# Local attention's weighted sums of V: from VectorE products and halvings to TensorE matmuls with softmax weights laid out as bands

## The chip, the cores and the metric

The kernel runs on one core of a Trainium2 chip. The metric is the device time of one execution in microseconds. Times of profiled executions come with a trace, from which the profile is made; TensorE's granted clock is 1.000 in the profile of the kernel before.

## The reference, cut to what matters

The output is a gated mix of two branches that read the same input `x` of 2048 tokens by 1024 features, in bf16.

```python
g = _sigmoid((x * gate_w).sum(-1, keepdims=True))
a = _A_ref(x, A_wqkv, A_wo)        # local dilated attention
b = _B_ref(x, B_w_gate, B_w_up, B_w_down)   # gelu(x w_gate) * (x w_up), then w_down
return g * a + (1 - g) * b
```

The attention has 32 heads of 32 features. Token s attends to 8 positions: s, s-2, s-4, ..., s-14.

```python
qkv = ... (x @ wqkv) ...           # q, k, v: [B, H, S, Dh]
W, dil = 8, 2
idx = pos[:, None] - off[None, :]  # off = 0, 2, ..., 14; positions below 0 are masked
logits = jnp.einsum("bhsd,bhswd->bhsw", q, kg) * scale
attn = _softmax(logits, axis=-1)
o = jnp.einsum("bhsw,bhswd->bhsd", attn, vg)   # the weighted sums of V
return o.transpose(...).reshape(B, S, D) @ wo
```

The hidden width of the second branch is 3584.

## The kernel before

The program is one long static order of instructions for each engine. It works on two halves of 1024 tokens (`s` = 0, 1), each of two chunks of 512. Large products are made by a seven-product scheme (Strassen-Winograd) over 2 x 2 blocks: of the contraction (two halves of 512 features), of the output rows and of the two chunks.

The middle of the program is a list of 78 **units** (class `Unit`). A unit makes seven block products, each of four matmuls of 512 columns (`mm`, L366), and moves the partial sums on with ScalarE copies (L384, L389, L396, L374, L372) and one VectorE addition (L403). In the order of the loop at L1249 a unit's slot is: its first product (`p1`), two products of the unit before (`p73`), its fifth product (`p5`), what is queued for the slot (`slotq`, `pre`), then the second and sixth products (`p26`), and the last product of the unit before (`p4`). Then the loop hands VectorE work to the slot from a list of background tasks by priority (`run_bg`, with a credit of 4.7 or 4.8 us a slot by estimated costs). `at(n, ...)` ties work to the start of a slot, `due` ends a task by a slot.

The units are, in order: two for gate and up (numbers 0 and 1), 16 for Q and K (2 to 17), 8 for V (18 to 25), and 52 for gate and up (26 to 77). After them comes `down`, the product of both branches with `w_down` and `wo`, once for each half.

- **Q and K.** Features lie on partitions; the weights' columns are taken with a step of 8 (`qk_forms`), so that the 32 heads lie on 32 partitions four times over. VectorE multiplies q with eight shifted views of k (`qk_mult`, L598); TensorE sums over each head's features with a matrix of ones (`reduce_mm`, L603): matmuls of 32 columns of weights which go to the four column groups of the array, 32 partitions of output each. The last 256 tokens of each half are spilled to HBM and done later (`spill`, L649). Softmax runs in blocks of 256 tokens on VectorE and ScalarE (`softmax`, `softmax_exp`, `softmax_back`), the gate is multiplied in, and the weights go to HBM (`w_d`, L712).
- **V.** `v_forms` takes the weights' columns with a step of 8 or 4 as the stationary operand and x as the streamed one: V comes out with features on partitions, tokens along the free axis, and is stored to `v_d` (`store_v`, L356).
- **Weighted sums** (`pv_all`, a background task of VectorE). For each of 8 blocks of 256 tokens `pv_load` fetches the block's weights, spread to all 128 partitions (L720), and V with 16 tokens of halo (L723). For each of 8 feature tiles one product of 128 x 2048 (L745), and for each pair of tiles three halving additions (L752), of 2048, 1024 and 512 elements. The result goes to HBM (`o_d`, L775).
- **Down projection.** `down` reads h and o back from HBM, scales by the gate (L918), combines blocks on VectorE (L927, L1004, L1012) and multiplies on TensorE (L1046, matmuls of 256 columns; L1079, of 512). Its early loads and scalings are `pre_down_0` to `pre_down_4`. In the kernel before, the load of the block `A12` is issued by `pv_all` in its last block, and `pre_down_2` when `pv_all` has ended.

Work on VectorE outside the weighted sums, in the same stretch: sums of the gate and up weights (L323), L403, and h = gelu(gate) * up (L254).

Of the kernel before, what the change touches and what calls it, by code (L numbers as in the profile page):

```python
# [52 lines left out]
R_O = (36, 32)  # L53
R_VB = (40, 48.25)
R_AB = (44.25, 52.5)
R_PROD2 = 56.5
# [7 lines left out]
def _win_ap(src: bass.AP, dims):  # L64
    return AP(src.tensor, src.offset, [list(src.ap[0])] + [list(d) for d in dims])
# [3 lines left out]
def kernel(  # L69
# [40 lines left out]
    def reg4(kb, a, b, c):  # L110
        return reg(kb, a * b * c).rearrange("p (a b c) -> p a b c", a=a, b=b)
# [11 lines left out]
    v_d = tc.dram_tile([P, NT, HALO + S], BF16, name="v_d")  # L123
# [8 lines left out]
    w_d = tc.dram_tile([NBLK, 32, NJ, SC], BF16, name="w_d")  # L132
# [4 lines left out]
    with tc.manual_schedule(engines={mybir.EngineType.PE, mybir.EngineType.DVE, mybir.EngineType.Activation,  # L137
# [195 lines left out]
        nc.gpsimd.dma_start(out=v_d[:, :, 0:HALO], in_=zh)  # L333
# [20 lines left out]
        def store_v(T, t, s):  # L354
            for i in range(2):
                nc.gpsimd.dma_start(out=v_d[:, t + 4 * i, HALO + s * SUP:HALO + (s + 1) * SUP], in_=T[:, i, :])  # L356
# [3 lines left out]
        class Unit:  # L360
            def __init__(self, L, f, kind, dst, fin=None, pre=None):
                self.L, self.f, self.kind, self.dst, self.fin, self.pre = L, f, kind, dst, fin, pre

            def mm(self, ps, form, rhs, start):
                for kt in range(HK):
                    self.pe = nc.tensor.matmul(ps, lhsT=self.L[form](kt), rhs=rhs[:, kt, :],  # L366
                                               start=(start and kt == 0), stop=(kt == HK - 1),
                                               skip_group_check=not start)
# [164 lines left out]
        wv4 = wv.rearrange("p k (c t) -> p k c t", t=NT)  # L533
        sv = [reg4(R_WV + 16 + 4 * i, HK, P, 4) for i in range(3)]
# [5 lines left out]

        def sums_v():
            L11, L12 = wv4[:, 0:HK, :, 0:4], wv4[:, HK:KT, :, 0:4]
            L21, L22 = wv4[:, 0:HK, :, 4:8], wv4[:, HK:KT, :, 4:8]
            for o_, a, b_, op in ((sv[0], L21, L22, ALU.add), (sv[1], sv[0], L11, ALU.subtract),
                                  (sv[2], L12, sv[1], ALU.subtract), (L21, L11, L21, ALU.subtract)):
                TT(out=o_, in0=a, in1=b_, op=op)
                yield 1.14

        def v_forms(t):
            r = lambda k0, tt: (lambda kt: _win_ap(wv[:, k0 + kt, tt:tt + 1], [[NT, P]]))  # L550
            z = lambda a: (lambda kt: _win_ap(a[:, kt, 0, t:t + 1], [[4, P]]))
            return {"L11": r(0, t), "L12": r(HK, t), "S3": r(0, t + 4), "L22": r(HK, t + 4),
                    "S1": z(sv[0]), "S2": z(sv[1]), "S4": z(sv[2])}

        for s in range(2):
            for t in range(4):
                u = add_unit(v_forms(t), xf[s], "qkv", st_first if s + t == 0 else st_tile)
                u.fin = lambda u=u, t=t, s=s: store_v(u.T, t, s)
# [17 lines left out]
        vb = [reg3(R_VB[i], NT, KV) for i in range(2)]  # L576
# [4 lines left out]
        ab_ = [reg4(R_AB[i], NJ, NWIN, SJ) for i in range(2)]  # L581
        ob_ = [reg3(R_O[i], NT, AC) for i in range(2)]
        prod2 = [reg4(R_PROD2 + 8 * i, 2, NJ, NWIN * SJ) for i in range(2)]

# [82 lines left out]
        def spill_reduce(s, accs):  # L667
            for g, acc in enumerate(accs):
                reduce_mm(bank(LGB + s), acc, g == 0, g == len(accs) - 1)
            bg(softmax(s * BPS + BPS - 1, 1, LGB + s, 3 + s), 1, now[0])  # L670
# [29 lines left out]
        def softmax_back(a, cnt, ee, e4, sw, m, bc):  # L700
            while a // BPS not in gated:
                yield None
            d = m
            V.tensor_reduce(out=d, in_=sw, axis=AX.X, op=ALU.add)
            yield 0.9 * cnt + 0.05
            V.reciprocal(out=d, in_=d)
            TT(out=d, in0=d, in1=gblk[:, a:a + cnt, :], op=ALU.mult)
            yield 0.65 * cnt
            TT(out=attn_all[:, a:a + cnt, :].rearrange("p a (w s) -> p a w s", w=NWIN), in0=e4, in1=bc(d), op=ALU.mult)
            yield 0.55 * cnt + 0.05  # L710
            for j in range(NJ):
                nc.gpsimd.dma_start(out=w_d[a:a + cnt, :, j, :].rearrange("a h n -> h a n"),  # L712
                                    in_=attn_all[32 * j:32 * j + 32, a:a + cnt, :])
            ready.update(range(a, a + cnt))
            if a == 2 * BPS - 1:
                two[0] = True

        def pv_load(a, i):
            src = w_d[a].rearrange("h j n -> h (j n)")
            nc.sync.dma_start(out=ab_[i % 2].rearrange("p j w s -> p (j w s)"),  # L720
                              in_=AP(src.tensor, src.offset,
                                     [[NJ * SC, 32], [0, 4], [1, NJ * SC]]))
            nc.sync.dma_start(out=vb[i % 2], in_=v_d[:, :, a * AC:a * AC + KV])  # L723

        PVO = (0, 1, 2, 4, 5, 6, 3, 7)

        def pv_all():
            for k in (0, 1):
                while PVO[k] not in ready:
                    yield None  # L730
            pv_load(PVO[0], 0)
            yield None
            for i, a in enumerate(PVO):
                if i + 1 < NBLK:
                    while PVO[i + 1] not in ready:
                        yield None
                    pv_load(PVO[i + 1], i + 1)
                if i == 0:
                    pv_task[0].prio = 5
                    tasks.sort(key=lambda t_: t_.prio)  # L740
                    yield None
                v, ab, o_ = vb[i % 2], ab_[i % 2], ob_[i % 2]

                def mult(t):
                    TT(out=prod2[(t // 2) % 2][:, t % 2], in0=ab,  # L745
                       in1=_win_ap(v[:, t, HALO:HALO + AC], [[SJ, NJ], [-DIL, NWIN], [1, SJ]]), op=ALU.mult)

                def fold(t, w):
                    pr = prod2[(t // 2) % 2]
                    h = lambda k: pr[:, :, :, k * w * SJ:(k + 1) * w * SJ]  # L750
                    out_ = h(0) if w > 1 else o_[:, t:t + 2, :].rearrange("p t (j s) -> p t j s", j=NJ)
                    TT(out=out_, in0=h(0), in1=h(1), op=ALU.add)  # L752

                mult(0)
                yield 1.14
                mult(1)
                yield 1.14
                for t in range(0, NT, 2):
                    if i + 1 == NBLK and t == 2:
                        load_A(Bs(0)["A12"], 0, 1, 0, 0, KX, False)  # L760
                    nxt = t + 2 < NT
                    if nxt:
                        mult(t + 2)
                        yield 1.14
                    fold(t, 4)
                    yield 1.14
                    if nxt:
                        mult(t + 3)
                        yield 1.14
                    fold(t, 2)  # L770
                    yield 0.68
                    fold(t, 1)
                    yield 0.4
                a0 = a % BPS % 2 * AC
                nc.gpsimd.dma_start(out=o_d[a // BPS][a % BPS // 2][:, :, a0:a0 + AC], in_=o_)  # L775
            while now[0] < n - 6:
                yield None
            pre_down_2(0)
# [28 lines left out]
        bg(spill(0), 4, QE + 2)  # L807
        bg(spill(1), 4, QE + 2)
        pv_task = [bg(pv_all(), 4.2, QE + 3)]
# [11 lines left out]
        def r_parts(half, nh, i0=0, i1=NK):  # L821
            ns = slice(nh * SC, (nh + 1) * SC)
            if i0 < NH_:
                e = min(i1, NH_)
                yield slice(i0, e), B_w_down[:, ns].rearrange("(i two p) n -> p i two n", two=2, p=P)[:, i0:e, half, :]
            if i1 > NH_:
                a = max(i0, NH_)
                yield slice(a, i1), A_wo[:, ns].rearrange("(p t) n -> p t n", t=NT)[:, 4 * half + a - NH_:4 * half + i1 - NH_, :]
# [403 lines left out]
        at(n - 7, lambda: pre_down_1(0))  # L1232
        at(NX0 + 3, lambda: pd.get("end") and pre_down_3(0))
# [15 lines left out]
        for b in range(n):  # L1249
# [13 lines left out]
            for fn in pre.pop(b, []):  # L1263
                fn()
                extra += 0.6
            cur.p26()
# [7 lines left out]
            if b == n - 1:  # L1274
                pre_down_4(0)
        assert not hooks and not pre and not post and not slotq, (hooks.keys(), pre.keys(), post.keys())
# [31 lines left out]
```

## Time and profile before

| | us |
|---|---|
| median of 3 runs | 720.37 (720.34 to 720.45) |
| the profiled execution | 720.06 |
| its span, first to last instruction | 718.3 |
| TensorE busy (matmuls) | 707.2 |
| VectorE busy | 673.2 |
| ScalarE busy | 328.7 |
| GpSimd busy | 134.5 |

In the profile, PE is TensorE's matmuls and PEld its weight loads, which overlap them; DVE is VectorE, ACT is ScalarE, POOL is GpSimd, SP is SyncE, which issues DMAs only. A group's line has the source line, engine, operation, output and input names, sizes, count, then busy us and mean ns of one, then the engine's idle time before them and what ended it. A line of the timeline has the start, the time taken, and in brackets the idle time before. Matmuls are pipelined: one of 512 columns is listed with 379 ns but the next starts 216 ns later. Durations are of the one profiled execution.

### The profile page before, as it was taken

How to read it: one execution, taken by the hardware profiler on the slowest of the kernel's cores; microseconds unless marked ns; L12 is line 12 of the kernel's file. 1: busy time of each engine (PE TensorE's matmuls, PEld its weight loads, DVE VectorE, ACT ScalarE, POOL GpSimd, SP SyncE). 2: the span in 40 equal slices, each digit the busy share in tenths (PEclk: the TensorE clock that was granted, in tenths of full speed). 3: DMA queues.
4: the chain of work that ended last, by engine and by line, in shares of the span. 5: the costliest groups of instructions: out<-in, count | busy, mean ns of one | idle time of the engine just before them, and what ended most of it. 6: DMA issues, size and time to landing. Idle time of an engine off the chain costs nothing. (4 is left out here: it accounts for less than half of the span.)

```text
span 718.3 us, 10752 instructions
## 1 busy us (share of the span) xinstructions
PE 707.2 (98%) x4051; PEld 408.2 (57%) x4107; DVE 673.2 (94%) x722; ACT 328.7 (46%) x600; POOL 134.5 (19%) x233
## 2 busy tenths in 40 slices
PE   8999999999999999999999999999999999999998
PEld 4466656655544444444444444444447886758887
DVE  2789989999999999999999999999999999899997
ACT  4554546444456665555555555555322321131431
POOL 1323544133210332121300000000210002110011
PEclk9999999999999999999999999999999999999999
DMA  9976643378264758574934836371891899995951
GB/s 276 284 183 219 229 142 122 106 247 304 102 205 127 231 197 252 175 221 149 294 115 152 280 123 214 124 288 59 300 427 52 307 401 396 420 429 223 379 213 60
DMA packets 92276, 162.04 MB, mean 226 GB/s; under 512 B 19280, under 2 KB 68848, under 8 KB 87872
## 3 DMA queue, kind: packets, MB, share of 16 engines
q1 hardware_dynamic: 75520, 105.46, 42.7%
q0 software_dynamic: 15984, 48.29, 19.3%
q10 hardware_dynamic: 720, 7.60, 2.7%
q8 instruction: 32, 0.52, 0.3%
q14 instruction: 20, 0.16, 0.1%
HBM read 112.17 MB, written 54.14 MB: 232 GB/s over the span
## 5 line engine op out<-in xcount | busy, mean ns | idle before, releaser
L366 PE MATMUL banks<-arena 128*128 128x512 bf16 x2136 | 472.1, 379 | 4.2 <-DVE arena L403 0.7
L366 PEld LDWEIGHTS <-arena 128*128 128x128 bf16 x2184 | 240.5, 111 | 235.3 <-issue 7.0
L1046 PE MATMUL banks<-arena 128*128 128x256 bf16 x1260 | 138.9, 273 | 0.8 <-DVE arena L1012 0.6
L1046 PEld LDWEIGHTS <-arena 128*128 128x128 bf16 x1260 | 123.1, 98 | 16.7 <-issue 1.5
L389 ACT COPY arena<-banks 128x512 f32<-128x512 f32 x78 | 45.8, 587 | 130.7 <-PE banks L366 130.7
L403 DVE TENSOR_TENSOR arena<-banks,arena 128x1024 bf16<-128x1024 f32 x78 | 95.2, 1221 | 11.0 <-PE banks L366 5.5
L374 ACT CAST arena<-banks 128x512 bf16<-128x512 f32 x102 | 59.7, 586 | 42.4 <-PE banks L366 42.4
L745 DVE TENSOR_TENSOR arena<-arena 128x2048 bf16<-128x2048 bf16 x64 | 77.0, 1220 | 0.5
L752 DVE TENSOR_TENSOR arena<-arena 128x2048 bf16<-128x2048 bf16 (+2 forms) x96 | 73.9, 776 | 1.0
L598 DVE TENSOR_TENSOR arena<-arena 128x2048 bf16<-128x2048 bf16 x64 | 74.7, 1219 | 0.1
L260 POOL DMA_DIRECT2D h_d<-arena x28 | 20.4, 730 | 226.5 <-DVE arena L254 195.4
L1079 PE MATMUL banks<-arena 128*128 128x512 bf16 x282 | 62.5, 379 | 0.3
L396 ACT COPY banks<-banks 128x512 f32<-128x512 f32 x78 | 44.5, 570 | 21.8 <-PE banks L366 20.0
L1004 DVE TENSOR_TENSOR arena<-arena 128x2304 bf16<-128x2304 bf16 x40 | 53.3, 1352 | 0.5
L384 ACT COPY banks<-banks 128x512 f32<-128x512 f32 x78 | 45.0, 576 | 13.6 <-PE banks L366 12.1
L1051 ACT COPY banks<-banks 128x256 f32<-128x256 f32 x60 | 21.4, 356 | 60.9 <-PE banks L1046 60.7
L1079 PEld LDWEIGHTS <-arena 128*128 128x128 bf16 x288 | 28.2, 98 | 33.5
L927 DVE TENSOR_TENSOR arena<-arena 128x2048 bf16<-128x2048 bf16 (+1 forms) x40 | 41.8, 1111 | 1.3 <-DMA arena<-h_d 1.3
L372 ACT ACTIVATE arena<-banks 128x512 bf16<-128x512 f32 x54 | 32.2, 597 | 15.4 <-PE banks L366 15.3
L323 DVE TENSOR_TENSOR arena<-arena 128x1024 bf16<-128x1024 bf16 x60 | 38.6, 685 | 0.5
L1012 DVE TENSOR_TENSOR arena<-arena 128x2304 bf16<-128x2304 bf16 x28 | 37.7, 1351 | 0.2
L254 DVE TENSOR_TENSOR arena<-arena 128x2048 bf16<-128x2048 bf16 x28 | 34.0, 1216 | 1.9 <-ACT arena L251 1.4
(93 smaller groups left out, 435.8 us busy)
## 6 DMA issues: line engine op xcount, KB each, us to landing
arena<-t_d SPq DMA_DIRECT2D x8, 2304.0 KB, 14.4
h_d<-arena POOLq DMA_DIRECT2D x28, 512.0 KB, 4.3
arena<-w_c SPq DMA_DIRECT2D x12, 1152.0 KB, 14.1
t_d<-arena POOLq DMA_DIRECT2D x36, 256.0 KB, 4.3
arena<-h_d SPq DMA_DIRECT2D x6, 1536.0 KB, 12.7
arena<-in_B_w_gate_dram SPq DMA_DIRECT2D x15, 512.0 KB, 5.7
arena<-in_B_w_up_dram SPq DMA_DIRECT2D x15, 512.0 KB, 5.3
arena<-in_B_w_down_dram SPq DMA_DIRECT2D x28, 256.0 KB, 6.6
```

The lines of the kernel that those rows point to most:

```text
L366: self.pe = nc.tensor.matmul(ps, lhsT=self.L[form](kt), rhs=rhs[:, kt, :], start=(start and kt == 0), stop=(kt == HK - 1), skip_group_chec ...
L374: nc.scalar.copy(out=o_, in_=i_)
L384: nc.scalar.copy(out=self.Y, in_=self.X)
L389: nc.scalar.copy(out=self.p5s, in_=self.V)
L396: nc.scalar.copy(out=self.Z, in_=self.Y)
L403: TT(out=self.T[:, :, c2s], in0=pair, in1=self.p5s.rearrange("p (o n) -> p o n", o=1).to_broadcast([P, 2, SC]), op=ALU.add)
L598: TT(out=dst, in0=q.rearrange("p (o s) -> p o s", o=1).to_broadcast([P, NWIN, AC]), in1=_win_ap(k, [[-DIL, NWIN], [1, AC]]), op=ALU.mult)
L745: TT(out=prod2[(t // 2) % 2][:, t % 2], in0=ab, in1=_win_ap(v[:, t, HALO:HALO + AC], [[SJ, NJ], [-DIL, NWIN], [1, SJ]]), op=ALU.mult)
L752: TT(out=out_, in0=h(0), in1=h(1), op=ALU.add)
L1004: TT(out=o_, in0=a, in1=b_, op=op)
L1046: nc.tensor.matmul(c(i, h, j), lhsT=l[:, kt, j * P:(j + 1) * P], rhs=r[:, kt, :], start=False, stop=(kt == KH - 1), skip_group_check=True)
L1079: nc.tensor.matmul(ps, lhsT=L[:, i, j * P:(j + 1) * P], rhs=R[:, i, :], start=(start and q == 0), stop=(q == NK - 1), skip_group_check=not ...
```

## The change

V is now formed with tokens on partitions: in the V units x is the stationary operand (128 tokens, `rows`) and the weights are streamed, 512 columns at a time, without a step. `v_d` becomes a table of tokens by 1024 features.

The weights of the softmax go to `w_d` in another order (eight pieces of 64 weights where there was one of 512, one DMA for each block and quarter), with a halo of zeros. The weighted sums are cut into windows of 114 queries (`BQ`), 9 for each half, 128 keys (`BK`) each. For one window:

- `pv_turn`: two transposes on TensorE bring the weights of 32 heads to keys on partitions (into bank 7); two ScalarE copies spread them over `ct`, with zeros between; a GpSimd DMA writes them to HBM so that each key's row is shifted by one query (`b_d`): the rows become a band matrix for each head, keys by queries, heads innermost.
- `pv_fetch`: three SP DMAs fetch the band's blocks of 38 queries, one fetches V of the 128 keys.
- `pv_mm`, twice: 16 matmuls each, one for each head. The stationary operand is V of that head, 128 keys by 32 features; the streamed operand is that head's column of the band, 114 queries, one bf16 from each 64 bytes. Four heads go to the four column groups. One ScalarE copy brings 16 heads' results to `o_all`, which goes to HBM by chunks of 512 tokens.

`pv_plan` lays this out over the units: from the slot in which the blocks 0 to 6 of weights are ready and the spills are done, which the code requires to be at least 35 slots before the ninth from the end. Windows come in pairs, one pair each three slots; in the first slot of three 32 matmuls, in the others 16 each. A window is turned five slots before its matmuls (the odd one of a pair: five before the odd one's first), and fetched three before. `pv_slot` stands in the loop between the fifth product of a unit and its second. The VectorE products and halvings, and their task, are gone. The loads of A12 and `pre_down_2` are tied to slots n - 8 and n - 6. Both spills now use one bank of PSUM for their reductions. The rows of `wo` are read in another order.

```diff
-    v_d = tc.dram_tile([P, NT, HALO + S], BF16, name="v_d")
+    v_d = tc.dram_tile([HALO + S, D], BF16, name="v_d")
...
+                    if self.rows is not None:
+                        l, r = r[:, self.rows * P:(self.rows + 1) * P], l
...
-        def pv_load(a, i):
...
-                def mult(t):
-                    TT(out=prod2[(t // 2) % 2][:, t % 2], in0=ab,
-                       in1=_win_ap(v[:, t, HALO:HALO + AC], [[SJ, NJ], [-DIL, NWIN], [1, SJ]]), op=ALU.mult)
...
-                    TT(out=out_, in0=h(0), in1=h(1), op=ALU.add)
...
+        def pv_turn(g):
+            s, i = wins[g]
+            K = rows(i) + HALO - DIL
+            ps = bank(7).bitcast(BF16)[:, 0:2 * P]
+            for h in range(2):
+                nc.tensor.transpose(out=ps[0:K, h * P:(h + 1) * P], in_=pt[s][h][:, BQ * i:BQ * i + K], identity=ident[:])
+            c = ct[g % 2]
+            for h in range(2):
+                nc.scalar.copy(out=_win_ap(c[0:K, 0, 16 * h:16 * h + 1], [[2 * 32, NWIN], [1, 16]]),
+                               in_=ps[0:K, h * P:(h + 1) * P].rearrange("k (w h) -> k w h", w=NWIN))
+            d = b_d[g % 3]
+            nc.gpsimd.dma_start(out=AP(d[:].tensor, d[:].offset, [[(BC + 1) * 32, K], [1, (2 * NWIN - 1) * 32]]), in_=flat(c[0:K]))
+
+        def pv_fetch(g):
+            s, i = wins[g]
+            n_ = rows(i)
+            for b in range(NSUB):
+                qa, qz = SQ * b, min(SQ * (b + 1), n_)
+                kz = qz + HALO - DIL
+                nc.sync.dma_start(out=band[g % 3][qa:kz, qa:qz, :],
+                                  in_=b_d[g % 3][qa:kz, qa + HALO - DIL:qz + HALO - DIL, :])
+            r0 = HALO + s * SUP + BQ * i - (HALO - DIL)
+            nc.sync.dma_start(out=vw[g % 3][0:n_ + HALO - DIL, :], in_=v_d[r0:r0 + n_ + HALO - DIL, :])
+
+        def pv_mm(g, e, bk):
+            s, i = wins[g]
+            n_, q0 = rows(i), BQ * i
+            K = n_ + HALO - DIL
+            b = bank(bk)
+            for t in range(4):
+                for c in range(4):
+                    h = 16 * e + 4 * t + c
+                    nc.tensor.matmul(b[32 * c:32 * c + 32, t * BQ:t * BQ + n_], lhsT=vw[g % 3][0:K, 32 * h:32 * h + 32],
+                                     rhs=_win_ap(band[g % 3][0:K, 0, h:h + 1], [[32, n_]]), start=True, stop=True,
+                                     skip_group_check=True)
+            nc.scalar.copy(out=o_all[:, 4 * e:4 * e + 4, q0:q0 + n_],
+                           in_=b[:, 0:4 * BQ].rearrange("p (t q) -> p t q", t=4)[:, :, 0:n_])
...
+        def pv_plan(b):
+            pv_put(b, pv_init)
+            pv_put(b + 2, lambda: pv_weights(0))
+            pv_put(b + 13, lambda: pv_weights(1))
+            for g in range(len(wins)):
+                u = b + 9 + 3 * (g // 2)
+                m0, m1, bk = (u + 1, u + 2, 6) if g % 2 else (u, u, 7)
+                pv_put(m0, lambda g=g: pv_mm(g, 0, 6))
+                pv_put(m1, lambda g=g, bk=bk: pv_mm(g, 1, bk))
+                pv_put(u - 5 + g % 2, lambda g=g: pv_turn(g))
+                pv_put(u - 3 + g % 2, lambda g=g: pv_fetch(g))
```

## The prediction

> **What bounds the kernel now.** I read the engine totals and groups on the profile's page first, then busy time by stretch, then the order of time in the stretch that the change edits. The totals, and the three groups that matter here:
>
> ```profile
> PE 707.2 (98%) x4051; PEld 408.2 (57%) x4107; DVE 673.2 (94%) x722; ACT 328.7 (46%) x600; POOL 134.5 (19%) x233
> L366 PE MATMUL banks<-arena 128*128 128x512 bf16 x2136 | 472.1, 379 | 4.2 <-DVE arena L403 0.7
> L745 DVE TENSOR_TENSOR arena<-arena 128x2048 bf16<-128x2048 bf16 x64 | 77.0, 1220 | 0.5
> L752 DVE TENSOR_TENSOR arena<-arena 128x2048 bf16<-128x2048 bf16 (+2 forms) x96 | 73.9, 776 | 1.0
> ```
>
> TensorE and VectorE both look full. The work that leaves VectorE is L745 and L752, 77.0 + 73.9 = 150.9 us. A busy share doesn't say which engine waits for the other, so I split the span where that work lies (its first product starts at 250.7 us, its last fold at 504.5 us), the hand-over to the down projection, and the down projection (busy us of each engine, then instructions):
>
> ```profile
> 254.00:500.00 246.00, 244.79 (x1119) 111.52 (x1140) 241.42 (x265) 138.01 (x226) 37.93 (x53) 1.00 0.57 186
> 500.00:545.00 45.00, 44.51 (x205) 20.37 (x208) 41.99 (x41) 12.44 (x23) 6.30 (x11) 1.00 0.80 313
> 545.00:718.30 173.30, 169.08 (x1399) 136.82 (x1401) 163.79 (x172) 46.99 (x115) 13.55 (x25) 1.00 0.74 295
> ```
>
> TensorE is busy 244.79 of 246 us: VectorE is full beside it, but nobody waits for it. The sharper test is the pace of the units, read from one ScalarE copy that each unit makes once (L389, start time first):
>
> ```profile
> 57.01 0.59 ACT L389 COPY arena<-banks 128x512 f32<-128x512 f32 x1 [1.97 <-PE banks L366]
> 63.05 0.59 ACT L389 COPY arena<-banks 128x512 f32<-128x512 f32 x1 [1.97 <-PE banks L366]
> 70.66 0.59 ACT L389 COPY arena<-banks 128x512 f32<-128x512 f32 x1 [1.97 <-PE banks L366]
> ...
> 210.62 0.59 ACT L389 COPY arena<-banks 128x512 f32<-128x512 f32 x1 [1.42 <-PE banks L366]
> 217.32 0.59 ACT L389 COPY arena<-banks 128x512 f32<-128x512 f32 x1 [1.97 <-PE banks L366]
> ...
> 332.93 0.59 ACT L389 COPY arena<-banks 128x512 f32<-128x512 f32 x1 [1.42 <-PE banks L366]
> 338.97 0.59 ACT L389 COPY arena<-banks 128x512 f32<-128x512 f32 x1 [1.97 <-PE banks L366]
> ```
>
> A unit is 28 matmuls of 512 columns, and it takes 6.04 us: 0.216 us a matmul, unit after unit, with VectorE's products beside it or not. Where extra matmuls are put between, the unit is longer by just them: 7.61 us with 24 reduction matmuls of L603 in it, 6.70 with 8. So the kernel is bound by TensorE's stream, and each matmul added to a unit is paid in full.
>
> **What is removed.** 150.9 us of VectorE between 250 and 505 us. TensorE's waits for VectorE that could come back are small: the waits in its timeline after 495 us are 0.28 us (510.16, for L403), 0.63 us (663.32) and 0.18 us (712.97), and the last two lie in the down projection, whose VectorE work is not touched. I credit 0.3 us. What is late next once VectorE is free is TensorE itself.
>
> **V with tokens on partitions.** The eight V units keep 28 matmuls of 512 columns; the two operands change places. Their weight loads stop stepping through `wv` (8 columns, 16 bytes). A weight load with that step (first row, units of Q and K) takes 143 ns, one without (second row, gate and up) 98:
>
> ```profile
> L366 PEld LDWEIGHTS <-arena x199: 142/143/171, 60.0 to 109.9; 128*128 128x128 bf16 x199
> L366 PEld LDWEIGHTS <-arena x927: 97/98/98, 299.9 to 499.8; 128*128 128x128 bf16 x186
> ```
>
> Both fit under a 216 ns matmul, and both kinds of unit take 6.04 us, so this is worth 0. The 16 stores of V stay 16, with pieces of 1 KB.
>
> **The weighted sums on TensorE.** There are 18 windows of 114 tokens (9 for each half), each with 32 heads: 576 matmuls of 128 rows by 32 columns, streaming 114 columns, in 144 sets of four that go to the four column groups. They run in 27 slots (three for each pair of windows), between the fifth product of a unit and the second. Three terms:
>
> (a) Entering and leaving. The nearest rows are L603's, the same shape of weights:
>
> ```profile
> 210.52 0.61 PE L603 MATMUL banks<-arena,ones_r 128*32 128x512 bf16 x8
> 211.06 30.52 PE L366 MATMUL banks<-arena 128*128 128x512 bf16 x137
> ```
>
> Eight of them lengthen the unit by 0.66 us. Two sets at the time of one matmul, 2 x 0.216 = 0.43, leave 0.23; 24 of them lengthen it by 1.57, and 6 x 0.216 = 1.30 leaves 0.27. So four column groups do run side by side, and a visit costs about 0.25 us. 27 visits: 6.75 us.
>
> (b) The 36 transposes. Sixteen of L213's took 1.07 us; less the last one's own 0.22 they stand 0.85/15 = 0.057 us apart: 36 x 0.057 = 2.1 us.
>
> ```profile
> 6.05 1.07 PE L213 MATMUL banks<-ident,arena 128*128 128x128 bf16 x16 [0.26 <-DVE arena L219]
> ```
>
> (c) The 144 sets. At L603's pace a set of 114 columns takes 114/512 x 0.216 = 0.05 us. But L603 streams runs of 64 neighbours, and the band is read at `[[32, n_]]`: one bf16 from each 64 bytes. No streamed operand of this kernel steps so. The nearest row is the strided weight load: 128 elements took 45 ns more, 0.35 ns each. If the four streams pay this independently, a set takes 0.05 + 114 x 0.00035 = 0.09 us; if they share one path to the memory, 0.05 + 456 x 0.00035 = 0.21; if they lose their concurrency besides, 4 x 0.09 = 0.36. I take 0.21: the row charges by the element read, and a set reads 456; and unstrided matmuls of about this size one after another, at the transposes' 0.057, come to the same, 0.23. 144 x 0.21 = 30.2 us. The ends 0.05 and 0.36 are kept: 7.2 and 51.8 us.
>
> [...]
>
> **What lies beside other work.** ScalarE gets 36 copies of about 456 elements (L389's 0.59 us for 512) and 36 small ones (at most that). A slot has at most 1.2 us of large ones, while ScalarE idles 1.42 to 1.97 us before L389 alone and its next evacuation must wait for four matmuls, 0.86 us, anyway. If that cover were gone they would cost up to 72 x 0.59 = 42 us; I take 0. SP loses 16 loads and gets 76 (72 band and V windows, 4 of weights); its two former ones took 0.54 and 0.95 us to issue, so some 50 us spread over 27 units. Behind them wait the gate and up weights, asked for three units before use. GpSimd gets 18 band stores, 12 more weight stores, zero fills and three band initialisations, loses 4 stores of the result, and is busy 19% now; the stores of h behind them are read only in the down projection. Each window has two units (12 us) from transpose to fetch and three (18 us) from fetch to matmul; before, a V load landed in 5.4 us and a weight store in 1.8 to 3.1. I take 0 for waits. The spare reduction bank that the second spill loses is free for some 30 us by then: 0. The loads of A12 and A22 leave the VectorE task for fixed units and land under TensorE as before: 0.
>
> **The sum.** 6.75 + 2.1 + 30.2 - 0.3 = 38.8 us. The profiled execution took 720.06 us (span 718.3 and 1.76 around it), 0.3 below the median of the runs: 720.06 + 38.8 = 758.9, and I say 759.
>
> **Rivals.** First, the stride costs nothing or little (0.05 to 0.09 us a set): 7.2 to 13.0 + 8.55 = 15.8 to 21.5 us, 736 to 742. For it: TensorE has hidden every operand read so far. Against: the 143 ns.
> Second, strided streams also lose concurrency: 0.36 a set, 51.8 + 8.55 = 60 us, 780 and above. For it: nothing shown runs four strided streams. Against: four streams run fully side by side in L603.
> Third, pairs of weight load and matmul can't be issued fast enough. At the transposes' 0.057 us a pair that is 576 x 0.057 = 32.8 + 8.55, 761 us, which the forecast's own band holds. [...]
> Fourth, a band lands late and TensorE stands: over 18 us from fetch to matmul, 18 windows by a few us each, 780 to 800. Against: the 5.4 us.
> Fifth, faster: VectorE's freed 150.9 us would have to pull TensorE's remaining gaps in. Their place is 254 to 718.3 us, and the three stretches above leave 1.2 + 0.5 + 4.2 = 5.9 us in all, so 714 us at the very best. It decides only if the added matmuls cost less than 5.9 us together, and the 27 visits alone cost 6.75; they would have to run beside the full-array ones, and L603 shows that they don't.
>
> **Numbers.** Forecast, 0.15 to 0.28 us a set, the issue rival in it: 0.52, with a range of its own from 750 to 769. Little stride cost: 0.25. Lost concurrency: 0.15. Late bands: 0.05. Faster: 0.02; within 0.2% (1.4 us, about what a measurement can tell from no change): 0.01. The range takes in the low rival whole and the high one at its price: 736 to 781; beyond it are the late bands and more than 0.36 us a set. Slower by over 0.2%: 0.97.
>
> **What would show it.** Units with windows spaced about 7.9, 7.2 and 7.2 us in turn (6.04 + 0.25 + 8 or 4 sets at 0.21 + transposes), all others at 6.04; VectorE's total near 522 us; the down projection as long as before. The set's time is in the starts of the new matmuls: 0.21 apart by fours. I am wrong if they stand at 0.05 to 0.09 or 0.36, if TensorE idles for a band's DMA or a ScalarE copy, or if units outside the 27 slots change their pace.

## The result, and the profile after

| | us |
|---|---|
| after, median | 762.34 (762.16 to 763.9) |
| before, median of the runs beside it | 720.36 (719.89 to 720.45) |
| ratio | 1.0589, 95% interval 1.0571 to 1.0607 |
| span of the profiled execution | 760.5 (before 718.3) |

Two executions are left out of every time and ratio below, one of `e8_waits` at 4354.54 us, which is its only profiled one, and one of the kernel before at 954.86 us.

The change costs 42.0 us. 759 was forecast, with a range from 736 to 781. The page of the changed kernel, its totals, the units' matmuls (L381, before L366) and the new ones (L783; a second form, because the ninth window of each half has 112 queries and not 114):

```profile
PE 743.9 (98%) x4651; PEld 415.2 (55%) x4719; DVE 532.3 (70%) x562; ACT 354.3 (47%) x672; POOL 165.1 (22%) x271
L381 PE MATMUL banks<-arena 128*128 128x512 bf16 x2125 | 476.8, 379 | 8.2 <-DVE arena L417 2.8
L783 PE MATMUL banks<-arena 128*32 128x114 bf16 (+1 forms) x576 | 34.2, 381 | 0.0
```

VectorE has lost 141 us of busy time and TensorE has gained 37; the span has followed TensorE. (VectorE's records of neighbouring instructions overlap by some 0.08 us, so that 160 instructions fewer take 141 us out of the total, not their groups' 150.9.) Busy time by stretch shows the same thing at the place of the change (columns PE, PEld, DVE, ACT, POOL, then clock, DMA share, GB/s):

```profile
254.00:500.00 246.00, 241.80 (x1536) 108.03 (x1565) 85.99 (x92) 140.62 (x260) 44.74 (x67) 1.00 0.66 210
500.00:545.00 45.00, 44.79 (x206) 20.42 (x209) 21.88 (x21) 25.65 (x43) 2.85 (x4) 1.00 0.60 208
588.00:760.50 172.50, 168.25 (x1392) 136.05 (x1393) 161.86 (x170) 46.16 (x114) 13.45 (x25) 1.00 0.74 297
```

From 254 to 500 us VectorE works 86 us where it worked 241, and TensorE is as full as ever; but the same 246 us now hold fewer units. The down projection behind the hand-over, last row, is as long as before. The units' pace is read from the same ScalarE copy (L403, before L389), its start in the first column:

```profile
293.90 0.58 ACT L403 COPY arena<-banks 128x512 f32<-128x512 f32 x1 [1.97 <-PE banks L381]
300.06 0.59 ACT L403 COPY arena<-banks 128x512 f32<-128x512 f32 x1 [1.43 <-PE banks L381]
308.00 0.60 ACT L403 COPY arena<-banks 128x512 f32<-128x512 f32 x1 [1.97 <-PE banks L381]
315.16 0.60 ACT L403 COPY arena<-banks 128x512 f32<-128x512 f32 x1 [1.43 <-PE banks L381]
```

A unit with two transposes takes 6.16 us, one with 32 of the new matmuls 7.94, one with 16 and two transposes 7.16. The timeline of TensorE shows these visits (start, time taken, count):

```profile
299.95 1.86 PE L783 MATMUL banks<-arena 128*32 128x114 bf16 x32
307.90 0.96 PE L783 MATMUL banks<-arena 128*32 128x114 bf16 x16
308.79 0.28 PE L756 MATMUL banks<-ident,arena 128*128 128x128 bf16 x2
```

Within a visit four matmuls start together and the next four 0.203 us later (median of the starts in the trace). The prediction took waits as nothing, and there are some of TensorE at three places, 4.9 us together, here with the idle time in brackets:

```profile
258.02 3.61 PE L381 MATMUL banks<-arena 128*128 128x512 bf16 x15 [1.22 <-ACT arena L388]
261.85 6.20 PE L381 MATMUL banks<-arena 128*128 128x512 bf16 x28 [0.22 <-ACT banks L398]
269.24 0.23 PE L756 MATMUL banks<-ident,arena 128*128 128x128 bf16 x1 [1.13 <-DMA arena<-w_d]
552.34 2.75 PE L381 MATMUL banks<-arena 128*128 128x512 bf16 x11 [2.29 <-DVE arena L417]
```

### The profile page after: what moved, and what is told of

It is laid out like the page before. It is cut to its first block, busy times and chain, and to the rows that moved or that the text cites. A ratio compares the mean times of both kernels' runs of the same rounds, so it can differ in the third digit from the quotient of the medians.

```text
span 760.5 us, 12049 instructions
## 1 busy us (share of the span) xinstructions
PE 743.9 (98%) x4651; PEld 415.2 (55%) x4719; DVE 532.3 (70%) x562; ACT 354.3 (47%) x672; POOL 165.1 (22%) x271
## 3 DMA queue, kind: packets, MB, share of 16 engines
q0 software_dynamic: 17664, 53.34, 20.4%
## 5 line engine op out<-in xcount | busy, mean ns | idle before, releaser
L381 PE MATMUL banks<-arena 128*128 128x512 bf16 x2125 | 476.8, 379 | 8.2 <-DVE arena L417 2.8
L381 PEld LDWEIGHTS <-arena 128*128 128x128 bf16 x2184 | 231.2, 107 | 244.3 <-issue 16.3
L417 DVE TENSOR_TENSOR arena<-banks,arena 128x1024 bf16<-128x1024 f32 x78 | 95.4, 1223 | 188.7 <-PE banks L381 99.8
L1083 PEld LDWEIGHTS <-arena 128*128 128x128 bf16 x1260 | 123.1, 98 | 16.6 <-issue 1.3
L403 ACT COPY arena<-banks 128x512 f32<-128x512 f32 x78 | 46.1, 591 | 130.4 <-PE banks L381 130.4
L388 ACT CAST arena<-banks 128x512 bf16<-128x512 f32 x102 | 59.6, 585 | 44.7 <-PE banks L381 42.2
L612 DVE TENSOR_TENSOR arena<-arena 128x2048 bf16<-128x2048 bf16 x64 | 74.6, 1218 | 0.1
L1116 PEld LDWEIGHTS <-arena 128*128 128x128 bf16 x288 | 28.2, 98 | 33.5
L964 DVE TENSOR_TENSOR arena<-arena 128x2048 bf16<-128x2048 bf16 (+1 forms) x40 | 41.7, 1109 | 0.0
L262 DVE TENSOR_TENSOR arena<-arena 128x2048 bf16<-128x2048 bf16 x28 | 34.1, 1216 | 4.2 <-ACT arena L388 2.8
L783 PE MATMUL banks<-arena 128*32 128x114 bf16 (+1 forms) x576 | 34.2, 381 | 0.0
L762 POOL DMA_DIRECT2D b_d<-arena x18 | 10.3, 572 | 108.3 <-ACT arena L759 98.2
```

The source lines that it names most:

```text
L381: self.pe = nc.tensor.matmul(ps, lhsT=l, rhs=r, start=(start and kt == 0), stop=(kt == HK - 1), skip_group_check=not start)
L388: nc.scalar.copy(out=o_, in_=i_)
L403: nc.scalar.copy(out=self.p5s, in_=self.V)
L417: TT(out=self.T[:, :, c2s], in0=pair, in1=self.p5s.rearrange("p (o n) -> p o n", o=1).to_broadcast([P, 2, SC]), op=ALU.add)
L612: TT(out=dst, in0=q.rearrange("p (o s) -> p o s", o=1).to_broadcast([P, NWIN, AC]), in1=_win_ap(k, [[-DIL, NWIN], [1, AC]]), op=ALU.mult)
L964: TT(out=f(o_), in0=f(a), in1=f(b), op=op)
```

## The experiments

Two questions were open. The size was right, but was it right for the reason given, that the band is streamed with a step of 64 bytes and four streams share one path? And is freed VectorE time worth nothing?

**Neighbours in the place of the step** (`e1_contig`).

```diff
-  rhs=_win_ap(band[g % 3][0:K, 0, h:h + 1], [[32, n_]]), ...
+  rhs=flat(band[g % 3])[0:K, BQ * h:BQ * h + n_], ...
```

> The streamed operand of the 576 small matmuls is 114 neighbouring elements of the band instead of one element from each 64 bytes; the values it multiplies are other ones, and nothing else is changed. Theory (the step through the band costs, and four streams share one path): a set of four falls from 0.205 us to 0.05 to 0.10, so 144 x 0.105 to 0.155 = 15 to 22 us less, 740 to 747 us. Rival (pairs of weight load and matmul are issued no faster than 0.05 us): sets stay at 0.2 us, 762 us. Rival (the four column groups don't run side by side at 114 columns): 4 x 0.05 = 0.2, also 762.

Measured: 741.97 us, ratio to before 1.030 (1.0284 to 1.0315). TensorE's timeline of this run:

```profile
300.14 0.58 PE L783 MATMUL banks<-arena 128*32 128x114 bf16 x32
306.81 0.38 PE L783 MATMUL banks<-arena 128*32 128x114 bf16 x16
```

The same 32 matmuls take 0.58 us, not 1.86; sets start 0.050 us apart. The step costs 20.4 us of the 42 by the times, and 144 x (0.203 - 0.050) = 22.0 by the starts; the four executions of this run lie up to 1.8 us apart. Both rivals, slow issue and no concurrency, fall.

**Steps of 8, 16 and 4 bytes** (`e2_step8b`, `e3_step16b`, `e11_step4b`): in the same place `[[4, n_]]`, `[[8, n_]]` and `[[2, n_]]`.

> As the run with neighbours, but every fourth element (8 bytes apart, other values). Theory with a price for each element read off the sequence: as with 64 bytes, 0.205 us a set, 762 us. Theory with a price for each 16-byte line: two elements share one, 228 lines x 0.00035 + 0.05 = 0.13 us a set, 751 us. [...] Issue rival: 762 us.

> As before with every eighth element (16 bytes apart, other values). Theory (price by element or by 16-byte line): as with 64 bytes, 0.2 us a set, 762 us. Rival (the price grows with the step, or comes from 64-byte steps alone): under 755 us.

> As the runs with steps of 8 and 16 bytes, with every second element (4 bytes, four elements on a 16-byte line; other values). So far a set took 0.050 us with neighbours, 0.104 at 8 bytes and 0.203 at 16 and at 64 bytes, which is one line of 16 bytes per 1.67 ns for each stream. By that, four elements on a line take 0.42 ns each and the step costs nothing: 0.05 us a set, 741 to 743 us. Rival (each doubling of the step costs): 0.07 us a set, 745 us; rival (any step loses): 750 us.

| step | time, us (median of 4, 2, 2, 2 and 4 executions) | a set, ns (median of the starts in the trace) |
|---|---|---|
| neighbours (2 bytes) | 741.97 | 50 |
| 4 bytes | 742.38 | 54 |
| 8 bytes | 750.37 | 104 |
| 16 bytes | 763.96 | 203 |
| 64 bytes (the changed kernel) | 762.34 | 203 |

At these steps the price goes as if by lines of 16 bytes. With eight or four elements on a line the step costs next to nothing (50 and 54 ns); two run at half pace (104), one at a quarter (203); and 64 bytes cost no more than 16 (203 for both; nothing in between was run). 114 elements in 0.19 us (0.193 with one stream, next experiment) are one line for each 1.67 ns. Two elements on a line are not enough to escape the price: 104 ns against 50.

**One column group** (`e4_onegroup`, with the step; `e10_onegroup_contig`, with neighbours).

```diff
-  nc.tensor.matmul(b[32 * c:32 * c + 32, t * BQ:t * BQ + n_], ...
+  nc.tensor.matmul(b[0:32, t * BQ:t * BQ + n_], ...
```

> All 576 small matmuls write the first column group, so that no two can run side by side; the step of 64 bytes stays, and the other three groups' results are left out. Theory (one shared path that reads one strided element each 0.35 to 0.45 ns, which is the bound of a set): the path is as full with one stream as with four, 4 x 0.05 = 0.2 us a set, 760 to 768 us. Rival (each stream pays its own step, 0.09 us a matmul, and four run side by side): 0.36 a set or more, 784 us. Rival (a strided stream takes 0.2 us by itself and four overlap fully): 0.8 us a set, 848 us.

> The control of the run with one column group: again all 576 small matmuls write the first column group, but each streams 114 neighbouring elements (other values). In the run with one group and the step a matmul followed the next after 0.193 us. If that is the step's price alone (1.67 ns a column, and a strided stream takes 0.19 us by itself), neighbours bring it to 0.050 to 0.057 us: 0.2 to 0.23 us a set, 762 to 767 us. If one group by itself is slow (weight loads that can't hide behind a matmul of the same group, 0.1 us and more), 800 to 870 us.

Measured: 872.02 us (ratio 1.2105, 1.2085 to 1.2126) and 763.52 us. The timelines, first with the step, then with neighbours:

```profile
301.71 6.35 PE L783 MATMUL banks<-arena 128*32 128x114 bf16 x32
315.07 3.25 PE L783 MATMUL banks<-arena 128*32 128x114 bf16 x16
```

```profile
300.15 1.83 PE L783 MATMUL banks<-arena 128*32 128x114 bf16 x32
308.06 1.00 PE L783 MATMUL banks<-arena 128*32 128x114 bf16 x16
```

By itself a strided matmul takes 0.193 us, one with neighbours 0.052. So the theory of a shared path falls. One strided stream is nearly as slow alone as four are together: each stream pays for its own lines, and four column groups run side by side with next to no loss, at 0.203 a set against 4 x 0.193, and at 0.050 against 4 x 0.052. It was the third case of the expectation. By the sets, 762.3 + 144 x (0.773 - 0.203) is 844 us. The other 28 us fit a lower clock: from 290 to 600 us of that profile the granted clock was 0.88 to 0.94.

```profile
290.00:340.00 50.00, 49.62 (x237) 24.22 (x238) 14.44 (x16) 20.42 (x41) 9.45 (x14) 0.94 0.54 169
340.00:400.00 60.00, 59.35 (x254) 27.08 (x259) 10.88 (x11) 23.51 (x46) 8.35 (x12) 0.88 0.44 135
400.00:500.00 100.00, 99.08 (x441) 46.67 (x448) 21.67 (x22) 36.87 (x71) 9.37 (x15) 0.90 0.38 115
500.00:600.00 100.00, 99.03 (x436) 46.36 (x443) 23.04 (x25) 37.10 (x65) 5.39 (x8) 0.91 0.38 123
```

What these stretches lack of the full clock, 50 x 0.06 + 60 x 0.12 + 100 x 0.10 + 100 x 0.09, is 29 us, an estimate of the loss that takes all work there as slowed alike; how much fell on the new matmuls was not shown. One column group alone doesn't bring this about: with neighbours (`e10_onegroup_contig`), where a visit of 32 takes 1.83 us and not 6.35, the granted clock was 1.00 over the whole profile.

**VectorE freed by itself** (`e6_no_sums`, then `e12_no_mm`). The first try left out transposes, matmuls and copies, and filled the result on VectorE:

```diff
         def pv_init():
+            V.memset(o_all, 0.0)
```

> VectorE freed by itself: the transposes, the small matmuls and the ScalarE copies of the windows are left out, the result of the attention is a constant, and all DMAs and zero fills stay. Theory (TensorE is the bound, and freeing VectorE gives nothing): 720.1 as before the change, plus the two waits that stay, 1.4 us behind GpSimd's zero fills and 2.3 us at the hand-over to the down projection: 721 to 724 us. Rival (VectorE's freed 151 us pull TensorE's gaps in): under 718 us.

Measured: 729.0 us, above both. The fill is one VectorE instruction of 3.47 us (second line, VectorE's timeline: L739); a unit's addition (L417) came late behind it, and TensorE stood for 3.69 us (first line, TensorE's timeline):

```profile
254.16 262.81 PE L381 MATMUL banks<-arena 128*128 128x512 bf16 x1180 [3.69 <-DVE arena L417]
```

```profile
243.72 3.47 DVE L739 MEMSET arena<- 128x4096 uint32 x1 [0.80 <-PE banks L381]
```

In the 5.64 us behind that stop the granted clock was 0.50, which is another 2.8 us by estimate (5.64 x 0.50):

```profile
254.16:259.80 5.64, 5.64 (x14) 2.01 (x14) 1.24 (x2) 3.53 (x5) 1.62 (x3) 0.50 1.00 352
```

With the wait of 2.29 us at the hand-over, 720.2 + 3.7 + 2.8 + 2.3 = 729.0: nothing is gained, but a result that rests on such corrections decides little. The second try left the fill out, kept transposes and copies, and had the edits of the next experiment against the three waits:

```diff
-            for t in range(4):
-                for c in range(4):
...
-                    nc.tensor.matmul(b[32 * c:32 * c + 32, ...
```

> VectorE freed by itself once more, without the zero fill of the earlier try, which held VectorE for 3.5 us at once and stopped TensorE: the kernel with its three waits taken away, without the 576 small matmuls; transposes, ScalarE copies (of what the banks hold), DMAs and fills stay. The attention's result is left out. Theory (VectorE's freed 151 us are worth nothing): 720.2 + 36 transposes x 0.057 = 722.3, within 721 to 724 us. Rival (they pull TensorE's gaps in, up to 5.9 us): 716 to 720 us.

Measured: 722.58 us, ratio 1.003 (1.0019 to 1.004), 2.3 us above the kernel before. That is the price forecast for the 36 transposes, 2.1, but two smaller things hide in it. TensorE still waits once, for 0.90 us (below), and the two waits for VectorE of 0.28 and 0.18 us that the kernel before has behind 495 us are gone. By this sum, 2.1 + 0.9 - 2.3, VectorE's freed 151 us are worth 0.7 us, which is no more than the interval leaves open, and not the 5.9 of the rival:

```profile
273.10 0.27 PE L756 MATMUL banks<-ident,arena 128*128 128x128 bf16 x2 [0.90 <-ACT arena L759]
```

**The three waits** (`e8_waits`). `pv_init_band` fills and writes one band, where `pv_init` did three at once.

```diff
+            for k in range(3):
+                pv_put(b + 2 * k, lambda k=k: pv_init_band(k))
...
-                pv_put(u - 5 + g % 2, lambda g=g: pv_turn(g))
+                pv_put(u - 4 if g == 0 else u - 5 + g % 2, lambda g=g: pv_turn(g))
...
-            bg(scale_task(Bs(s)["A21"], s, 1, 0, KX), 6, n - 2)
+            bg(scale_task(Bs(s)["A21"], s, 1, 0, KX), 6, n - 5)
```

> The changed kernel with its three waits taken away: the band's zero fills on GpSimd spread over three slots, the first window's transposes one slot later, the scaling of A21 allowed three units earlier. Theory (1.4, 1.1 and 2.3 us of TensorE's idle time were placement): 757 to 759 us. Rival (the waits come back elsewhere): 761 us and above.

Measured: 758.8 us (758.05 to 759.56), ratio 1.0533 (1.0519 to 1.0547): 3.6 us of the expected 3 to 5. The traces of `e12_no_mm` and `e9_both`, which have the same edits, show what became of the waits. Those behind the fills and at the hand-over are gone. The one at the first window's transposes has changed its cause: they now stand in one slot with the second window's, in the same bank, and these wait 0.90 us for ScalarE's copies (line above).

How the first wait came about can be followed in the changed kernel's timelines: GpSimd fills the bands for 9.4 us (L740), the store of an h tile stands behind it, and ScalarE waits for that store before it can use the tile again (L388). The store was issued at 247.75 us, 3.9 later than in the kernel before. It also took 9.6 us to land where it had taken 5.2: the three stores of the bands, 912 KB each, had been issued just ahead of it. The edit spreads fills and stores alike, so their shares are not separated.

```profile
236.03 9.40 POOL L740 MEMSET arena<- 128x3648 bf16 x3
```

```profile
257.39 0.58 ACT L388 CAST arena<-banks 128x512 bf16<-128x512 f32 x1 [2.54 <-DMA h_d<-arena]
```

The last one comes of the freed time itself. With no products left in the list, the list gives the slot the next tasks, three scalings of A21 (L955); VectorE first stands for 2.79 us until ScalarE has delivered (L262), and then works them off in the fixed order ahead of the addition that TensorE waits for (L417):

```profile
545.52 1.23 DVE L262 TENSOR_TENSOR arena<-arena 128x2048 bf16<-128x2048 bf16 x1 [2.79 <-ACT arena L388]
546.78 1.23 DVE L265 TENSOR_TENSOR arena<-arena,omgrep 128x2048 bf16<-128x2048 bf16 x1
547.92 3.22 DVE L955 TENSOR_TENSOR arena<-arena,omgrep 128x2048 bf16<-128x2048 bf16 x3
551.06 1.22 DVE L417 TENSOR_TENSOR arena<-banks,arena 128x1024 bf16<-128x1024 f32 x1
```

**A version that uses this** (`e9_both`, `e13_visits`). VectorE, idle there, lays each band out again with queries as neighbours; the edits of `e8_waits` are in. In the second version each window's 32 matmuls come in one slot (last pair of lines), and the four transposes of a pair of windows come in one slot, in two banks.

```diff
+        def pv_repack(g):
+            for h0 in range(0, 32, 8):
+                V.tensor_copy(out=pk[g % 2][0:K, h0:h0 + 8, 0:n_],
+                              in_=band[g % 2][0:K, 0:n_, h0:h0 + 8].rearrange("k q h -> k h q"))
...
-                                     rhs=_win_ap(band[g % 3][0:K, 0, h:h + 1], [[32, n_]]), ...
+                                     rhs=pk[g % 2][0:K, h, 0:n_], ...
...
-                m0, m1, bk = (u + 1, u + 2, 6) if g % 2 else (u, u, 7)
+                m0, m1, bk = (u + 1, u + 1, 7) if g % 2 else (u, u, 7)
```

> A version that computes everything: the changed kernel with its three waits taken away, and VectorE, which is idle there, lays each window's band out again with queries as neighbours (four copies of 8 heads a window), so that the matmuls stream neighbours. Theory: 759.0 - 144 x (0.203 - 0.050) = 737 us, within 735 to 740. Rival (VectorE's copies delay the addition that each unit needs, or collide with other access): 742 us and above.

> The version with bands laid out again, and each window's 32 matmuls in one slot: 18 visits to the column groups in the place of 27, the four transposes of a pair in the third slot. Theory (a visit costs 0.25 us): 9 x 0.25 = 2.2 us less than with 27 visits, about 735 us. Rival (what a visit costs is hidden): the same as with 27. Neither theory has it below the kernel before, 720 us.

Measured: 736.01 us (ratio 1.0222, 1.0204 to 1.024) and 733.01 us (1.0175, 1.0162 to 1.0189). The first version's totals and its copies, and the first transposes in the first and in the second version:

```profile
PE 725.3 (99%) x4719; PEld 408.0 (56%) x4719; DVE 594.8 (81%) x634; ACT 350.8 (48%) x672; POOL 176.6 (24%) x270
L782 DVE COPY arena<-arena 128x912 bf16<-128x912 bf16 x64 | 57.6, 967 | 0.0
273.48 0.27 PE L759 MATMUL banks<-ident,arena 128*128 128x128 bf16 x2 [0.90 <-ACT arena L762]
273.89 0.39 PE L759 MATMUL banks<-ident,arena 128*128 128x128 bf16 x4
```

65 us of VectorE's idle time (the copies of the short windows add 7.0) buy 22.8 us of TensorE's, where 144 x (0.203 - 0.050) = 22.0 was expected. The second version is 3.0 us faster, but not by its nine visits fewer alone: with a second bank the wait of 0.90 us is gone too. That leaves 2.1 us, 0.23 for a visit, close to the 0.25 forecast. Neither version beats the kernel before: with 144 x 0.050 = 7.2 us of sets, 18 visits and the transposes, TensorE still carries 13 us more.

## Why the prediction was right or wrong, point by point

- **What bounds the kernel.** Right. `e12_no_mm` takes VectorE's 150.9 us away, gives TensorE the transposes alone, and is 2.3 us longer than before. VectorE's total was forecast near 522 us and is 532.3, by the overlap of the records.
- **V with tokens on partitions: 0.** The units of V keep their pace, 6.04 us in both kernels where no other matmul lies between.
- **(a) Visits, 6.75 us.** About right. In the units shown, 7.94 - 6.04 - 8 x 0.203 = 0.28 us, and 7.16 - 6.04 - 0.12 - 4 x 0.203 = 0.19; nine of the first and 18 of the second are 5.9 us, 0.22 each. The last experiment has 0.23. `e8_waits` less `e12_no_mm` is 36.2 us for sets and visits; less 144 x 0.203 = 29.2 that leaves 7.0, 0.26 each.
- **(b) Transposes, 2.1 us.** Right. A unit with two of them is 0.12 us longer, and 18 x 0.12 = 2.2. The 0.3 us credited for VectorE's waits were 0.5 (0.28 and 0.18).
- **(c) The sets, 30.2 us at 0.21.** The size was right: 0.203, 29.2 us. The step behind it was wrong: "0.35 ns each" by the strided weight load, shared by four streams. A strided element costs (0.193 - 0.050)/114, or 1.25 ns, more than a neighbour, and every stream pays by itself. The size was met by luck: the two faults cancelled, since 456 x 0.35 ns and 114 x 1.25 ns are nearly the same. The second support, unstrided pairs at 0.057 us one after another, fell too: with neighbours a set takes 0.050. With the same row and the other reading that the prediction offered, independent streams, it would have come out at 0.09 and 742 us. Why the 128 strided elements of a weight load cost 45 ns more and 114 streamed ones 143 ns more was not shown.
- **Cover, taken as 0.** Wrong, by the prediction's own sign that TensorE must not idle for ScalarE. Its waits at the start of the windows and at the hand-over are 4.9 us, of which `e8_waits` wins 3.6 back. They outweigh the 1.0 us by which the sets and the 0.9 by which the visits fell short of the forecast, so 762.3 was measured and not 759. GpSimd's fills were named with the stores of h behind them, and dismissed because h is read late; but the store also frees the tile, and ScalarE needs it. ScalarE's new copies, the other loads of SP and the bands' landings did stay hidden: only 1.13 us at the first window's transposes were a late load.
- **The rivals.** Little stride cost (736 to 742) is what `e1_contig` has with neighbours, 742: right in price, wrong for 64 bytes. Lost concurrency and slow issue are ruled out by its 0.050 us a set. No matmul of a window waited for a band. Faster is ruled out by `e12_no_mm`.

Read from the traces alone, the parts are 29.2 for the sets, 5.9 for the visits, 2.2 for the transposes, 4.9 for the waits, less 0.5 for VectorE's: 41.7 us, of 42.0.

## What to carry to other kernels

When one engine's stream sets the pace, taking work from its busy neighbour gains next to nothing (here 0.7 us or so for 151), and every matmul added is paid for (a unit of 6.04 us took 7.94 with 32 of them): look at the pace of a repeated unit, not at two busy shares. Lay a streamed operand out so that neighbours follow each other, or at least four bf16 lie on each 16 bytes (here 0.050 and 0.054 us a set, where one on each took 0.203); an idle engine can do it, and here it took 23 us off. Before work is added to a queue or a list that looks idle, ask who waits for what stands behind it: a store that nobody reads soon may still free a buffer (here ScalarE waited 2.54 us for one, and TensorE 1.22 behind it). And before a difference of two runs is put down to one edit, look in both traces for what else went away: here a wait of 0.90 us looked like a third of the price of nine visits.

## What the runs showed of the hardware that was not expected

- A streamed bf16 operand with two elements or fewer on a 16-byte line moved at one line for each 1.7 to 1.8 ns and stream, at steps of 8, 16 and 64 bytes (104, 203 and 203 ns for 57, 114 and 114 lines); four streams to four column groups did so at once, with little loss (0.203 us for four, 0.193 for one).
- Four small matmuls of 114 columns to four column groups, each with its own weight load, started every 0.050 us in `e1_contig`, which is 12.5 ns a pair of instructions.
- In `e4_onegroup` the granted clock fell though TensorE was listed as busy for 59.35 of 60 us: it was 0.88 over these 60 us, in which strided matmuls used one column group, up to 6.35 us at a time. With neighbours in the same column group, up to 1.83 us at a time, it was 1.00. After 3.69 us of idleness in `e6_no_sums` it was 0.50 for 5.64 us, so that the stop cost 6.5 us by estimate.
